# Streaming the recurrent layer's weight chunks from a contiguous DRAM copy

## The chip, the core and the metric

The kernel runs on one core of a Trainium2 chip. A time is the device time of one execution in microseconds; the time before is the median of three runs.

## The reference

Two independent parts are computed, and their outputs stand side by side in the last dimension. Part A is a shift of the keys, a long convolution by FFT, and gating. Part B, which the change touches, is a recurrent transformer: 2048 tokens in 64 segments of 32, each preceded by 8 memory tokens that the segment before has produced.

```python
for s in range(n_seg):                       # 64, strictly one after the other
    xs = x[:, s * seg_len:(s + 1) * seg_len, :]
    h = concatenate([mem, xs], axis=1)       # 40 tokens x 1024
    q, k, v = (einsum('btd,dhe->bhte', h, W) for W in (Wq, Wk, Wv))   # 32 heads x 128
    p = softmax(where(mask, q @ k.T * scale, -1e9))
    o = einsum('bhte,hed->btd', p @ v, Wo)
    mem = o[:, :8, :]                        # goes into the next segment
    outs.append(o[:, 8:, :])
```

The four weights have 1024 x 4096 elements each in bfloat16, 8 MB each and 32 MB together. They are used anew in every segment[...].

## The kernel before

`a_kernel` computes part A first, in three stages that pass data through DRAM tensors (SK1, SU1, SZ); its last stage loads `zt` tiles in turn from SP and from GpSimd (L381). Then comes `b_kernel`.

**Chunks.** The 32 MB of weights are cut into 64 chunks of 128 x 2048 elements, 512 KB each, in the order in which a segment uses them (`order`): Wk and Wq for the first half of the heads, Wk and Wq for the second, Wv for both, then Wo. A chunk of Wk, Wq or Wv is named (m, kc, g): 128 rows of the weight, and half g of its 4096 columns, so its 128 pieces of 4 KB lie 8 KB apart in DRAM. A chunk of Wo covers two heads, in pieces of 2 KB. Of the 64, 44 are resident: 18 in `Wearly` (loaded before the projection stage) and 26 in `Wlate` (loaded after it, L553). The other 20, spread evenly over the order, are *streamed*: in every segment they are fetched again from DRAM. They are 4 chunks of Wk, 6 of Wq, 5 of Wv and 5 of Wo.

**Where the stream reads.** `stream_src` (L430) gives the source. A streamed Wk, Wq or Wv chunk is read from the input itself. The five Wo chunks are first copied, in DRAM, to the scratch tensor WOS, one after the other and each contiguous (L439), by GpSimd at the very start of the run:

```python
    for i, ch in enumerate(ostream):
        nc.gpsimd.dma_start(WOS[i].rearrange("p (hh d) -> p hh d", hh=2), dram_chunk(ch))
```

**The projection stage** (L481 to L546) comes before the loop. It transposes x, and computes the keys, queries and values of the last 8 of each segment's 32 tokens for all segments at once, since these need no memory tokens, and stores them to the DRAM tensors REC and VBD. It needs Wk, Wq and Wv once in full. What is not in `Wearly` is loaded, 30 chunks in all, through the ring `pw` of ten buffers (`group`, L501). `Wlate` later takes the memory that this stage gives back.

**The segment loop** (from L590) has its order written out by hand. Projections (`Proj.run`, L649) and the output projection (`out_proj`, L735) take a resident chunk or the next one of the ring `wring`, which has four buffers. When PE has used a ring chunk, `done` calls `fetch` (L571), and SP issues the load of the chunk four places on in the stream:

```python
    def fetch():
        n = len(loaded)
        if n < len(uses):
            t = ring.tile([128, 2048], BF, tag="wring", name="wring")
            nc.sync.dma_start(t[:], stream_src(uses[n]))
            loaded.append(t)
```

So at most four fetches are under way, and one is issued only when a buffer comes free. GpSimd issues the segment's other transfers: its record `rec` (192 KB, L595), VBs (four of 16 KB, L622) and the outputs (L788, L793). After a segment PE transposes the new memory into the next one's input (L601, L602), and the next segment's projections start.

Of the kernel before, what the change touches and what calls it, by code (L numbers as in the profile page):

```python
# [9 lines left out]
BF = mybir.dt.bfloat16  # L10
# [11 lines left out]
NSTREAM = 20  # L22
NEARLY = 18
RING = 4


def a_kernel(ctx: ExitStack, tc, q, k, v, shift_k, ssm_k, ssm_D, outa, dbg_stop=None):
# [363 lines left out]
def b_kernel(ctx: ExitStack, tc, x, mem0, Wq, Wk, Wv, Wo, outb, n_seg):  # L391
    nc = tc.nc
# [11 lines left out]
    order = []  # L404
# [7 lines left out]
    streamed = set()  # L412
# [5 lines left out]
    late = resident[NEARLY:]  # L418


    ostream = [ch for ch in order if ch[0] == 3 and ch in streamed]

    def dram_chunk(ch):
        m, a, g = ch
        return Wo_v[a] if m == 3 else W_v[m][a, g]

    def dst_view(ap, ch):
        return ap.rearrange("p (hh d) -> p hh d", hh=2) if ch[0] == 3 else ap

    def stream_src(ch):  # L430
        return WOS[ostream.index(ch)] if ch[0] == 3 else dram_chunk(ch)

    dram = ctx.enter_context(tc.tile_pool(name="b_dram", bufs=1, space=DRAM))

    REC = dram.tile([128, n_seg, 768], BF, name="REC")
    VBD = dram.tile([n_seg, 4, 8, 1024], BF, name="VBD")
    WOS = dram.tile([max(1, len(ostream)), 128, 2048], BF, name="WOS")
    for i, ch in enumerate(ostream):
        nc.gpsimd.dma_start(WOS[i].rearrange("p (hh d) -> p hh d", hh=2), dram_chunk(ch))  # L439

    const = ctx.enter_context(tc.tile_pool(name="b_const", bufs=1))
    ident = const.tile([128, 128], BF, name="ident")
# [38 lines left out]
    with ExitStack() as c0:  # L481
        xp = c0.enter_context(tc.tile_pool(name="b0_x", bufs=3))
        xtp = c0.enter_context(tc.tile_pool(name="b0_xt", bufs=1))
        pring = c0.enter_context(tc.tile_pool(name="b0_ring", bufs=5))
        st = c0.enter_context(tc.tile_pool(name="b0_st", bufs=2))
        ps0 = c0.enter_context(tc.tile_pool(name="b0_ps", bufs=4, space=PSUM))
        ps0t = c0.enter_context(tc.tile_pool(name="b0_pst", bufs=2, space=PSUM))
        XT_all = xtp.tile([128, n_seg, 8, SEG], BF, name="XT_all")
        XBT = xtp.tile([128, 8, n_seg, 8], BF, name="XBT")
        for b in range(n_blk):  # L490
            X_sb = xp.tile([128, 1024], BF, tag="X_sb", name="X_sb")
            (nc.sync if b % 2 == 0 else nc.scalar).dma_start(X_sb[:], x[b * 128:(b + 1) * 128, :])
            tp = ps0t.tile([128, 1024], BF, tag="tp0", name="xt_ps")
            for kc in range(8):
                nc.tensor.transpose(tp[:, kc * 128:(kc + 1) * 128], X_sb[:, kc * 128:(kc + 1) * 128], ident[:])
            tpv = tp[:].rearrange("p (k j t) -> p j k t", k=8, j=4)
            nc.vector.tensor_copy(XT_all[:, 4 * b:4 * b + 4], tpv)
            nc.scalar.copy(XBT[:, :, 4 * b:4 * b + 4, :].rearrange("p k j t -> p j k t"), tpv[:, :, :, NX:SEG])  # L498
        nc.sync.dma_start(REC[:, :, 0:256], XT_all[:].rearrange("p s k t -> p s (k t)"))

        def group(m, g):  # L501
            ws = []
            for kc in range(8):
                ch = (m, kc, g)
                if ch in res:
                    ws.append(res[ch])
                else:
                    t = pring.tile([128, 2048], BF, tag="pw", bufs=10, name="pw")
                    nc.sync.dma_start(t[:], dram_chunk(ch))
                    ws.append(t[:])  # L510
            return ws

        flip = [0]

        def evac(dst, src):
            flip[0] ^= 1
            if flip[0]:
                nc.scalar.copy(dst, src)
            else:
                nc.vector.tensor_copy(dst, src)  # L520

        for m in (0, 1):
            for g in range(2):
                ws = group(m, g)
                stage = st.tile([128, n_seg, 16, 8], BF, tag="stage", name="stage")
                for hl in range(16):
                    ps = ps0.tile([128, 512], F32, tag="ps0", name="kb_ps")
                    for kc in range(8):
                        nc.tensor.matmul(ps[:], lhsT=ws[kc][:, hl * 128:(hl + 1) * 128],  # L529
                                         rhs=XBT[:, kc].rearrange("p s t -> p (s t)"),  # L530
                                         start=(kc == 0), stop=(kc == 7))
                    evac(stage[:, :, hl, :], ps[:].rearrange("p (s t) -> p s t", t=8))
                o = 256 * (m + 1) + 128 * g
                nc.sync.dma_start(REC[:, :, o:o + 128], stage[:].rearrange("p s h t -> p s (h t)"))
        for g in range(2):
            ws = group(2, g)
            for tb in range(4):
                vst = st.tile([128, 4, 512], BF, tag="vst", name="vst")
                for c in range(4):
                    ps = ps0.tile([128, 512], F32, tag="ps0", name="vb_ps")  # L540
                    for kc in range(8):
                        nc.tensor.matmul(ps[:], lhsT=XBT[:, kc, 16 * tb:16 * tb + 16, :].rearrange("p s t -> p (s t)"),
                                         rhs=ws[kc][:, c * 512:(c + 1) * 512], start=(kc == 0), stop=(kc == 7))
                    evac(vst[:, c, :], ps[:])
                for c in range(4):
                    nc.sync.dma_start(VBD[16 * tb:16 * tb + 16, c, :, g * 512:(g + 1) * 512], vst[:, c, :])  # L546
# [4 lines left out]
    for i, ch in enumerate(late):  # L551
        res[ch] = wlate_t[:, i, :]
        (nc.sync if i % 2 == 0 else nc.scalar).dma_start(dst_view(res[ch], ch), dram_chunk(ch))  # L553
    ring = ctx.enter_context(tc.tile_pool(name="b_ring", bufs=RING))
    one = ctx.enter_context(tc.tile_pool(name="b_one", bufs=1))
# [11 lines left out]
# [6 lines that stand above are left out]
# [33 lines left out]
    with tc.manual_schedule():  # L606
        for _ in range(RING):
            fetch()
# [190 lines left out]
def kernel(  # L799
# [24 lines left out]
    with ExitStack() as ctx_b:  # L824
        b_kernel(ctx_b, tc, B_x[0], B_mem0[0],
                 B_Wq.rearrange("d h e -> d (h e)"), B_Wk.rearrange("d h e -> d (h e)"),
                 B_Wv.rearrange("d h e -> d (h e)"), B_Wo.rearrange("h e d -> (h e) d"),
                 outb, n_seg)
# [35 lines left out]
```

## Time and profile before

| what | value |
|---|---|
| time, median of 3 runs | 2768.48 us (2750.39 to 2782.67) |
| span of the profiled execution | 2752.4 us |
| part A and the start, to about | 335 us |
| projection stage, from about 335 to | 526 us |
| Wlate loads and segment loop, from 526 us to | 2752 us |
| ring fetches | 1280, 512 KB each |
| HBM read, written | 777.14 MB, 54.00 MB |
| mean granted TensorE clock | 0.897 |

The page cuts the span in 40 slices of 68.8 us. For each slice it gives the busy share of each engine in tenths, and for the 16 DMA engines together their mean busy share and the GB/s that they moved. A wait is listed as the engine that sat idle, the tile and line of the instruction it then started, and what released it. "PE acc L649 <- DMA wring<-in_B_Wq_dram" is PE before a projection matmul, waiting for a ring chunk that comes from Wq. Ring fetches landed this long after their issue, by source: Wq 5.6 us, Wv 5.9, WOS 6.0, Wk 6.2 (medians).

### The profile page before, as it was taken

Reading aid. Unit: us, or ns where it says so; the run is one execution under the profiler, and the core shown is the slowest. Engines: PE = TensorE matmul, PEld = TensorE weight load, DVE = VectorE, ACT = ScalarE, POOL = GpSimd, SP = SyncE. Lnnn points to the kernel's source line nnn. Section 1 sums busy time; section 2 is a strip of 40 time slices with the busy share of each in tenths; the row PEclk is TensorE's granted clock in tenths of the full one; section 3 lists DMA queues with packets and bytes.
Section 4 is the critical chain, followed back from the end, with each engine's and each line's share of the span. In section 5 each row is a group of like instructions: output and inputs, shape, how many; then the busy total and the mean of one; then the engine's idle time right before and its main releaser. Section 6 shows DMA issues by size and latency. Waiting matters only on the chain. (4 is left out here: it accounts for less than half of the span.)

```text
span 2752.4 us, 76238 instructions
## 1 busy us (share of the span) xinstructions
PE 1851.6 (67%) x33620; PEld 910.9 (33%) x33620; DVE 662.9 (24%) x1944; ACT 639.9 (23%) x1143; POOL 454.2 (17%) x1195
## 2 busy tenths in 40 slices
PE   3565398556676777666666676667666767666766
PEld 1221243223333333333333333333333333333333
DVE  5896221111211111111111111111111111111111
ACT  6872111012222111112111111121212111111111
POOL 4043000001111111111111211121212111111111
PEclk9897599879999888998989988999998998998988
DMA  7986845699999998999999998999999998999897
GB/s 267 308 286 245 311 114 159 210 338 329 329 331 332 323 317 311 322 325 320 318 312 322 324 316 310 331 319 318 330 317 333 316 324 302 329 316 325 304 317 258
DMA packets 300164, 833.65 MB, mean 303 GB/s; under 512 B 72156, under 2 KB 84476, under 8 KB 299831
## 3 DMA queue, kind: packets, MB, share of 16 engines
q1 hardware_dynamic: 265560, 767.19, 79.9%
q0 software_dynamic: 23888, 37.39, 4.2%
q10 hardware_dynamic: 10384, 24.20, 2.6%
q8 instruction: 262, 4.29, 0.6%
q14 instruction: 70, 0.57, 0.1%
HBM read 777.14 MB, written 54.00 MB: 302 GB/s over the span
## 5 line engine op out<-in xcount | busy, mean ns | idle before, releaser
L649 PE MATMUL acc<-wring,rec 128*32 128x512 bf16 x3840 | 419.9, 425 | 455.5 <-DMA wring<-in_B_Wq_dram 261.0
L649 PEld LDWEIGHTS <-rec 128*32 128x32 bf16 x12288 | 341.0, 102 | 932.9 <-issue 727.9
L658 ACT CAST qkv_sb<-acc 128x512 bf16<-128x512 f32 x384 | 225.1, 586 | 1143.8 <-PE acc L649 1095.7
L649 PE MATMUL acc<-Wearly,rec 128*32 128x512 bf16 x4608 | 425.8, 451 | 34.7 <-DVE rec L602 23.6
L649 PE MATMUL acc<-Wlate,rec 128*32 128x512 bf16 x3840 | 341.3, 399 | 0.0
L735 PEld LDWEIGHTS <-OT 128*32 128x32 bf16 x8192 | 250.0, 102 | 222.9 <-issue 203.7
L735 PE MATMUL yacc<-Wlate,OT 128*32 128x256 bf16 x5632 | 280.6, 292 | 11.4 <-issue 11.4
L735 PE MATMUL yacc<-wring,OT 128*32 128x256 bf16 x2560 | 154.1, 297 | 143.8 <-DMA wring<-WOS 139.8
L626 POOL COPY KT<-rec 128x128 bf16<-128x128 bf16 x128 | 38.4, 300 | 768.2 <-PE S L675 677.9
L749 DVE COPY KT<-qk_tp 128x512 bf16<-128x512 bf16 x64 | 27.2, 425 | 549.8 <-PE qk_tp L664 549.8
L595 POOL DMA_DIRECT2D rec<-REC x64 | 37.3, 583 | 701.8 <-PE acc L649 339.1
L788 POOL DMA_DIRECT2D out_dram<-Y x64 | 48.5, 758 | 545.8 <-ACT Y L785 514.4
L622 POOL DMA_DIRECT2D VBs<-VBD x256 | 129.4, 512 | 0.2
L680 DVE TENSOR_REDUCE mx<-S 128x5 f32<-128x200 f32 x128 | 47.1, 368 | 281.9 <-PE S L675 281.1
L717 ACT CAST OT<-OTp 128x512 bf16<-128x512 f32 x128 | 75.0, 586 | 152.0 <-PE OTp L708 150.1
L664 PE MATMUL qk_tp<-ident,qkv_sb 128*128 128x128 bf16 x1024 | 110.2, 235 | 0.0
L602 DVE COPY rec<-y_tp 128x64 bf16<-128x64 bf16 x64 | 12.3, 192 | 393.0 <-PE y_tp L601 378.0
L785 ACT CAST Y<-yacc 128x256 bf16<-128x256 f32 x64 | 23.8, 373 | 356.8 <-PE yacc L735 356.8
L664 PEld LDWEIGHTS <-qkv_sb 128*128 128x128 bf16 x1024 | 63.5, 103 | 113.8 <-issue 83.8
L735 PE MATMUL yacc<-Wlate,OTB 128*32 128x256 bf16 x1408 | 91.2, 276 | 11.7 <-issue 11.3
L721 DVE CAST OTB<-OTp 128x128 bf16<-128x128 f32 x128 | 34.8, 272 | 246.3 <-ACT OT L717 246.3
L529 PE MATMUL kb_ps<-XBT,Wearly 128*128 128x512 bf16 x288 | 84.3, 384 | 1.2 <-ACT XBT L498 1.2
(191 smaller groups left out, 2131.9 us busy)
## 6 DMA issues: line engine op xcount, KB each, us to landing
wring<-in_B_Wq_dram SPq DMA_DIRECT2D x384, 512.0 KB, 5.6
wring<-in_B_Wv_dram SPq DMA_DIRECT2D x320, 512.0 KB, 5.9
wring<-WOS SPq DMA_DIRECT2D x320, 512.0 KB, 6.0
wring<-in_B_Wk_dram SPq DMA_DIRECT2D x256, 512.0 KB, 6.2
rec<-REC POOLq DMA_DIRECT2D x64, 192.0 KB, 5.7
SK<-s_sb SPq DMA_DIRECT2D x16, 512.0 KB, 4.6
SU<-s_sb SPq DMA_DIRECT2D x16, 512.0 KB, 4.9
Kg<-SK ACTq DMA_DIRECT2D x32, 256.0 KB, 3.9
```

Source lines behind the costliest of these rows:

```text
L529: nc.tensor.matmul(ps[:], lhsT=ws[kc][:, hl * 128:(hl + 1) * 128], rhs=XBT[:, kc].rearrange("p s t -> p (s t)"), start=(kc == 0), stop=(kc ...
L595: nc.gpsimd.dma_start(rec[:], REC[:, s, :])
L622: nc.gpsimd.dma_start(VBs[32 * c:32 * c + 8, :], VBD[s, c])
L626: nc.gpsimd.tensor_copy(KT[:, :, :, 32:40], KBs[:, 128 * g:128 * g + 128].rearrange("p (c i t) -> p i c t", c=4, i=4))
L649: nc.tensor.matmul(self.acc[32 * c:32 * c + 32, :], lhsT=hT[:, kc, :], rhs=w[:, c * 512:(c + 1) * 512], start=(kc == 0), stop=(kc == 7), t ...
L658: nc.scalar.copy(sb[:], self.acc[:])
L664: nc.tensor.transpose(tp[:, i * 128:(i + 1) * 128], sb[:, i * 128:(i + 1) * 128], ident[:])
L680: nc.vector.tensor_reduce(out=mx[:], in_=S, op=ALU.max, axis=AX.X)
L717: nc.scalar.copy(OT[:], o_view(g)[:, :, :, 0:32])
L721: nc.vector.tensor_copy(OTB[:, :, 4 * g:4 * g + 4, 8 * j:8 * j + 8], o_view(g)[:, :, :, 32:40])
L735: nc.tensor.matmul(yacc[32 * dq:32 * dq + 32, o:o + 256], lhsT=src, rhs=w[:, hh * 1024 + dq * 256:hh * 1024 + (dq + 1) * 256], start=(h == ...
L788: nc.gpsimd.dma_start(bass.AP(outb.tensor, outb.offset + SEG * s * 2048, [[256, 4], [2048, 32], [1, 256]]), Y[:])
```

## The change

All 20 streamed chunks get a place in one DRAM scratch tensor, WS, each chunk contiguous, and the loop streams from there alone. The Wo chunks are copied as before, now to WS. The 15 chunks of Wk, Wq and Wv are copied on the side: all of them pass through the `pw` ring of the projection stage once, and when such a tile has landed GpSimd stores it to its place in WS. The point is that the 128 pieces of 4 KB of every fetch then lie back to back in DRAM, where before those of 15 chunks lay 8 KB apart. `PITCH`, the length of a row in WS, is 2048 elements, so that rows follow each other without a gap.

```diff
+PITCH = 2048
...
-    ostream = [ch for ch in order if ch[0] == 3 and ch in streamed]
+    ring_order = [ch for ch in order if ch in streamed]
...
     def stream_src(ch):
-        return WOS[ostream.index(ch)] if ch[0] == 3 else dram_chunk(ch)
+        return WS[ring_order.index(ch), :, 0:2048]
...
-    WOS = dram.tile([max(1, len(ostream)), 128, 2048], BF, name="WOS")
-    for i, ch in enumerate(ostream):
-        nc.gpsimd.dma_start(WOS[i].rearrange("p (hh d) -> p hh d", hh=2), dram_chunk(ch))
+    WS = dram.tile([len(ring_order), 128, PITCH], BF, name="WS")
+    for ch in ring_order:
+        if ch[0] == 3:
+            nc.gpsimd.dma_start(dst_view(stream_src(ch), ch), dram_chunk(ch))
...
                 else:
                     t = pring.tile([128, 2048], BF, tag="pw", bufs=10, name="pw")
                     nc.sync.dma_start(t[:], dram_chunk(ch))
+                    if ch in streamed:
+                        nc.gpsimd.dma_start(stream_src(ch), t[:])
                     ws.append(t[:])
```

## The prediction

> **What bounds the kernel now.** I read the busy line first, then the time slices, then the waits of the segment loop, and last the transfers of single stretches. The page says that no engine is full but the DMA engines nearly are from slice 9 on:
>
> ```profile
> PE 1851.6 (67%) x33620; PEld 910.9 (33%) x33620; DVE 662.9 (24%) x1944; ACT 639.9 (23%) x1143; POOL 454.2 (17%) x1195
> ...
> DMA  7986845699999998999999998999999998999897
> GB/s 267 308 286 245 311 114 159 210 338 329 329 331 332 323 317 311 322 325 320 318 312 322 324 316 310 331 319 318 330 317 333 316 324 302 329 316 325 304 317 258
> ```
>
> The loop of 64 segments runs from 559 us (first ring fetch) to the end. Issues of the ring's Wo chunks, which close each segment, start at 584.8 us for the first of them and 2732.9 us for the last, and one segment's burst of five takes about 7 us to issue: (2148.1 - 7) / 63 = 34.0 us a segment. The waits of PE alone from 600 to 2740 us (engine, line, tile, releaser: total us, times, longest):
>
> ```profile
> PE acc L649 <- DMA wring<-in_B_Wq_dram: 260.1, 248, 3.1
> PE yacc L735 <- DMA wring<-WOS: 136.3, 177, 2.5
> PE acc L649 <- DMA wring<-in_B_Wv_dram: 94.5, 139, 2.5
> PE acc L649 <- DMA wring<-in_B_Wk_dram: 60.5, 61, 3.2
> PE yacc L735 <- issue: 30.1, 25, 2.3
> ```
>
> The first four are one wait, for a ring chunk: 551.4 us over 63 segments, 8.8 us of each 34.0. With every chunk on time a segment would need about 25 us of PE, so PE does not end the segment; the stream of 20 chunks of 512 KB does. The page's chain that ended last holds 0% on every line and is of no use here.
>
> Next: is the stream equally fast from both kinds of source? Fifteen chunks of a segment come from Wk, Wq, Wv, as 128 pieces of 4 KB with 8 KB from one to the next (half of each row of 4096 columns). Five come from WOS, the same 4 KB pieces back to back. I took windows in seven segments, five of which are shown; columns are the stretch, its length, busy time of PE, PEld, DVE, ACT, POOL, granted clock, DMA share, GB/s. First the middle of the Wk/Wq/Wv stretch, then the WOS stretch of the same segments:
>
> ```profile
> 1273.00:1296.50 23.50, 16.21 (x292) 6.77 (x293) 4.94 (x17) 5.38 (x11) 4.54 (x15) 0.93 0.91 319
> 1305.80:1328.50 22.70, 15.56 (x300) 6.49 (x300) 4.49 (x15) 5.03 (x10) 4.54 (x15) 0.98 0.96 332
> 1339.30:1362.10 22.80, 16.83 (x308) 7.04 (x311) 4.51 (x15) 5.30 (x11) 4.54 (x15) 0.93 0.93 330
> 1410.40:1433.70 23.30, 16.38 (x300) 6.77 (x293) 5.24 (x18) 5.61 (x11) 4.54 (x15) 0.93 0.94 323
> 1444.20:1468.00 23.80, 16.65 (x298) 6.77 (x302) 4.56 (x16) 4.97 (x10) 4.28 (x15) 0.93 0.89 316
> ```
>
> ```profile
> 1297.90:1304.00 6.10, 4.23 (x132) 2.97 (x127) 0.29 (x1) 1.17 (x2) 0.59 (x1) 0.93 1.01 386
> 1329.90:1338.00 8.10, 6.39 (x160) 4.24 (x163) 0.51 (x3) 1.17 (x2) 0.57 (x1) 0.79 0.88 284
> 1363.80:1370.80 7.00, 5.03 (x188) 4.16 (x182) 0.35 (x2) 1.17 (x2) 0.59 (x1) 1.00 0.91 329
> 1435.20:1441.80 6.60, 5.41 (x148) 3.77 (x146) 0.29 (x1) 1.17 (x2) 0.59 (x1) 0.74 0.94 321
> 1470.00:1475.90 5.90, 3.34 (x123) 2.25 (x116) 0.29 (x1) 0.96 (x2) 0.58 (x1) 1.00 1.00 391
> ```
>
> The reader is to divide the last column by the one before: what the engines move while they are busy. Over all seven stretches it is 321 / 0.925 = 347 GB/s in the first kind and 347 / 0.952 = 365 GB/s in the second. The trace also keeps every DMA packet. In both kinds half of the 4 KB packets take 159 ns or less, but 10.9% of those from Wk/Wq/Wv take over 200 ns against 5.0% from WOS, so the means are 187.7 and 176.8 ns. The source in HBM, not the transfer's size, makes that tail.
>
> **What the Trainium skill says.** "DMA: Bandwidth & Descriptors", section "Latency and other measured facts", has large row pitches slow copies (207 GB/s at 512 KiB, 103 at 4 MiB) and advises padding or contiguous tiles. An 8 KiB pitch is not in its list; this trace agrees in direction and is far milder, 347 against 365. The same page, "Issuing engines are not separate DMA queues": transfers of all issuers interleave on the same 16 engines. Here the loads of zt, issued in turn by SP and by POOL, land in 6.9 and 6.7 us, which agrees; so copies issued by POOL are not free where the DMA share is high. "HBM Reference", "Specifications", puts a core that streams alone at about 425 GB/s, bounded by its engines; the best stretches here show 386 to 392 at full share, so contiguous WOS has little left above it.
>
> **The change part by part.** *The stream.* All 1280 fetches keep their size, order, queue (SP) and ring of four; only the source of 960 turns from pitched to contiguous. A chunk is 128 packets on 16 engines, 8 each. If the 15 pitched chunks take on the mean of WOS: 15 x 8 x (187.7 - 176.8) ns = 1.31 us of each engine's time a segment, 84 us over 64. From the windows: 15 chunks start on average 1.73 us apart, 25.9 us, and 25.9 x (1 - 347/365) = 1.28 us, or 82 us. I take 83. It comes out of PE's 8.8 us of waiting, so PE hides none of it.
>
> *The added copies.* Fifteen of the 30 pw tiles of the projection stage are also stored to WS by POOL, 15 x 512 KB = 7.9 MB. The Wo copies were there before and only change their target. In program order three stores stand between POOL's zt loads and twelve after the identity is made. Wherever the engines are full one costs 524 KB at 316 GB/s (the rate from 260 to 345 us) = 1.66 us. pw loads were issued from 239 to 321 us for ten tiles, eight of them streamed, in stretches with DMA shares of 0.95, 1.01 and 0.81; PE's transposes at 335 us wait for X_sb loads queued there. I charge six of these eight, 10 us. The other seven fall after 362 us, where shares are 0.42 to 0.61 and PE is busy: hidden, except beside the last Wv loads at 486 to 491 us, for which PE already waits 10.2 us once; two stores there, 3 us. Sum 13 us. Bounds: 0, and all fifteen exposed, 25 us.
>
> *The added waits.* A store waits for its pw load, and behind it on POOL stand zt loads, whose ring of four already makes POOL wait 2 to 7 us for PE, and later the first rec load, for which POOL sits idle 247 us: hidden. A pw slot is free only when its store has read it; stores end a few us after the load, the slot is asked for one matmul group (about 27 us) later: hidden. Wlate, which takes over that memory, is issued from 526 us, 35 us after the last pw load: hidden. The ring's first fetch from WS is at 559 us, after all stores.
>
> Sum: 2768.5 - 83 + 13 = 2698 us, 2.5% faster.
>
> **The rivals.**
> *It is the phase, not the layout.* WOS chunks are fetched while PE does the output projection, beside fewer other transfers. For: rec and VBs loads fall in the other stretch. Against: Wk/Wq/Wv packets that start with no POOL-issued packet within 0.3 us still average 187 ns, and with 12 to 19 packets under way, where nearly all of them start, those of WOS have the shorter tail at each number. Gain 0, cost 13: 2781 us.
> *It is the place in HBM.* Mean packets of the 15 pitched positions of a segment run from 172 to 198 ns though all have one pitch, so addresses matter and the new buffer's are unknown. If WS is no better than the weights, the five Wo chunks lose too: 5 x 8 x 10.9 ns x 64 = 28 us, 2768.5 + 28 + 13 = 2809 us, slower. Against: WOS is the same layout in the same pool, and all five of its chunks are at 175 to 180.
> *The ring hides half.* SP issues a fetch only when PE has released a slot, so engines already idle 8% of the loop and may idle more: 2768.5 - 42 + 13 = 2740 us. Against: PE still waits for data in most chunks.
> *More than the packets say.* Shorter tails make all engines of a chunk end together. If all chunks follow each other as WOS chunks do now (1.61 us apart), a segment is 32.2 us, 115 us less in all: 2667 us.
>
> **How the numbers follow.** Forecast 0.52; more gain 0.10; ring hides half 0.14; phase 0.12; place 0.12. The forecast spreads by some 35 us either way (the copy's bounds, the runs before spreading over 32 us). The range reaches from just under the larger gain to the phase case, 2655 to 2785; left out is most of the place case and a little at each end. Faster by over 1% is under 2741: nearly all of the forecast, the larger gain, half of the ring case, 0.66. Slower by over 1%: the place case and a part of the phase case, 0.15. The same: 0.19.
>
> **What would show it.** Right: 34.0 us a segment falls to 32.7; PE's wait for wring falls from 551 to about 470 us; GB/s over share in the first kind of stretch rises from 347 to about 365; the WOS kind stays; the first ring fetch moves from 559 to about 572 us. Wrong: packets from WS with the old tail (place or phase), a ring fetch starting 25 us or more late (copies exposed), or the share in the loop dropping below 0.90 with the segment unchanged (ring).

## The result, and the profile after

The changed kernel takes 2680.1 us (median of 4 runs, 2659.7 to 2688.4) against 2766.7 us (2750.4 to 2782.7) before: a ratio of 0.968, 95% interval 0.960 to 0.976. The profiled executions are 2752.4 and 2686.0 us long. The one before lies near the lower end of its runs and the one after is the slowest of its four, so the pair of traces shows 66 us of the 87.

The page's slices of the changed kernel (busy share of the DMA engines in tenths, GB/s) and the start of the chain that ended last, which this time reaches back through the loop (by engine, then by line; half of the span is the ring's transfers):

```profile
DMA  7886945599999999999999999998999999999996
GB/s 282 307 285 247 345 142 162 176 370 334 332 337 330 348 319 332 338 330 328 329 334 333 329 329 334 329 326 312 330 332 329 328 349 322 346 324 346 334 345 248
...
DMA 56%; PE 31%; issue 3%; DVE 3%; ACT 1%; POOL 1%; SPq 0%; DVEq 0%; ACTq 0%; POOLq 0%
DMA wring<-WS 50%; PE acc L654 14%; PE yacc L740 6%; PE kb_ps L534 4%; PE qk_tp L669 2%; PE vb_ps L547 2%; DMA out_dram<-ot 1%; DMA Wearly<-in_B_Wk_dram 1%; ACT Y L790 1%; DMA pw<-in_B_Wv_dram 1%; PE y_tp L606 1%; DMA X_sb<-in_B_x_dram 1%; POOL Yre L342 1%; DVE rec L607 0%; DMA Wlate<-in_B_Wv_dram 0%
```

PE's waits for the ring in the loop, 600 to 2740 us:

```profile
PE acc L654 <- DMA wring<-WS: 332.1, 393, 4.3
PE yacc L740 <- DMA wring<-WS: 152.6, 197, 2.3
```

They sum to 484.7 us, 66.7 less than the 551.4 before; nearly all of the 74 us by which 63 segments got shorter (below) was waiting for chunks. The projections gained 83 us of it. The output projection, whose source was contiguous before as well, waits 16 us longer.

The segment's length is read from the copy of the output Y, once a segment. From the profile's view of tile Y, kernel before, then after (count, ns min/median/max, first and last start in us):

```profile
L785 ACT CAST Y<-yacc x64: 372/373/373, 599.1 to 2740.6; 128x256 bf16<-128x256 f32 x64
```

```profile
L790 ACT CAST Y<-yacc x64: 372/372/373, 604.5 to 2672.3; 128x256 bf16<-128x256 f32 x64
```

Divided by 63: 33.99 and 32.82 us a segment, 1.17 us less, 75 us over 64. The first segment ends 5.4 us later. The window over the loop from 700 to 2500 us (columns as in the prediction), before and after:

```profile
700.00:2500.00 1800.00, 1255.06 (x26489) 632.47 (x26480) 336.30 (x1233) 359.58 (x689) 305.26 (x904) 0.91 0.92 321
```

```profile
700.00:2500.00 1800.00, 1293.06 (x27318) 646.56 (x27319) 347.54 (x1275) 371.49 (x713) 313.58 (x935) 0.91 0.94 332
```

The reader is to see that *two* columns have moved: GB/s by 3.4%, and the share with it. GB/s over share, the figure on which the prediction was built, only goes from 349 to 353. To see why, I counted from the trace's packet records, over segments 3 to 62, how many of the 16 engines were busy at each moment (the means of packets are those of all 64 segments; "PITCH 4096" is a kernel of the experiments, with the pieces of all twenty chunks 8 KB apart):

```
                          before   after   PITCH 4096
us a segment               34.0     32.8     35.5
mean 4 KB ring packet, ns  185      182      186
  Wk/Wq/Wv chunks          188      183      186
  Wo chunks                177      180      188
us with 13 to 15 busy      12.6      9.4     13.0
us with 8 to 12 busy        4.6      2.9      7.3
engine time lost, us        3.2      2.5      4.4
```

The last row sums, over all moments with under 16 packets, the idle engines' share of 16. Packets give 20 x 8 x 2.5 ns = 0.40 us of the 1.17; most of the rest, 3.2 - 2.5 = 0.7 us, is engines that no longer stand idle while others still work. I read this as transfers that finish raggedly: a chunk has landed only when the last of its packets is done, PE frees its buffer after that, and only then is the next fetch issued. No run tests this reading by itself. What the runs do show is that waiting for PE has a part in it: where no fetch waits for PE (the run with ring and computation apart, below), 0.7 us is lost per twenty chunks, not 2.5.

### The profile page after: what moved, and what is told of

The parts are those of the page before. It is cut to its first block, busy times and chain, and to the rows that moved or that the text cites. A ratio compares the mean times of both kernels' runs of the same rounds, so it can differ in the third digit from the quotient of the medians.

```text
span 2686.0 us, 76248 instructions
## 1 busy us (share of the span) xinstructions
PE 1844.0 (69%) x33598; PEld 904.9 (34%) x33620; DVE 659.9 (25%) x1944; ACT 639.8 (24%) x1143; POOL 461.6 (17%) x1210
## 4 chain that ended last, share of the span: by engine, by line
DMA 56%; PE 31%; issue 3%; DVE 3%; ACT 1%; POOL 1%; SPq 0%; DVEq 0%; ACTq 0%; POOLq 0%
DMA wring<-WS 50%; PE acc L654 14%; PE yacc L740 6%; PE kb_ps L534 4%; PE qk_tp L669 2%; PE vb_ps L547 2%; DMA out_dram<-ot 1%; DMA Wearly<-in_B_Wk_dram 1%; ACT Y L790 1%; DMA pw<-in_B_Wv_dram 1%; PE y_tp L606 1%; DMA X_sb<-in_B_x_dram 1%; POOL Yre L342 1%; DVE rec L607 0%; DMA Wlate<-in_B_Wv_dram 0%
## 5 line engine op out<-in xcount | busy, mean ns | idle before, releaser
L654 PE MATMUL acc<-Wearly,rec 128*32 128x512 bf16 x4608 | 436.0, 461 | 32.3 <-DVE rec L607 21.3
L654 PE MATMUL acc<-Wlate,rec 128*32 128x512 bf16 x3840 | 333.3, 390 | 0.0
L740 PEld LDWEIGHTS <-OT 128*32 128x32 bf16 x8192 | 235.5, 100 | 236.2 <-issue 220.1
L740 PE MATMUL yacc<-Wlate,OT 128*32 128x256 bf16 x5632 | 274.0, 286 | 13.0 <-issue 13.0
```

The source lines that it names most:

```text
L654: nc.tensor.matmul(self.acc[32 * c:32 * c + 32, :], lhsT=hT[:, kc, :], rhs=w[:, c * 512:(c + 1) * 512], start=(kc == 0), stop=(kc == 7), t ...
L740: nc.tensor.matmul(yacc[32 * dq:32 * dq + 32, o:o + 256], lhsT=src, rhs=w[:, hh * 1024 + dq * 256:hh * 1024 + (dq + 1) * 256], start=(h == ...
```

## The experiments

**Copies without their use.** All copies as in the changed kernel, but the loop reads Wk, Wq and Wv from the weights (`ws_place` is a chunk's place in WS, to which the copies still go; those lines are left out):

```diff
-        return WS[ring_order.index(ch), :, 0:2048]
+        return ws_place(ch) if ch[0] == 3 else dram_chunk(ch)
```

> All twenty chunks are copied to WS as in the changed kernel, but the loop streams Wk, Wq and Wv from the weights and only Wo from WS. Theory 1 (the gain is made where the loop reads; the copies only cost): a segment stays at 34.0 us, the first ring fetch comes at about 566 us instead of 559, time about 2774 us, ratio to before 1.000 to 1.006. Theory 2 (the copies themselves, or the changed start of the run, bring some of the gain): ratio clearly under 0.995.

Measured: 1.0043 (1.001 to 1.0077), a segment 34.2 us, Wk/Wq/Wv packets 187 ns. Theory 1 holds: the gain is made where the loop reads. The copies and their waits cost 0.4%, 12 us, and by the interval between 3 and 21. (The 0.2 us a segment by which this trace is longer than the one before, 13 us in all, is less than the runs of one kernel differ.)

**The same scratch, other pitches.** Three kernels changed only where rows of WS lie:

```diff
-PITCH = 2048
+PITCH = 4096
```

> The changed kernel with PITCH 4096: WS has the rows of 4 KB at 8 KB from one to the next, as in the weights, in the same scratch tensor. Theory 1 (it is the layout: pieces that follow each other read with a shorter tail): the gain is gone and the Wo chunks lose theirs too, time 2780 to 2810 us, ratio 1.005 to 1.015, mean 4 KB packet about 187 ns in both kinds. Theory 2 (it is the place: the scratch tensor lies better in HBM than the weights): ratio stays at about 0.968, packets 182 ns.

```diff
-PITCH = 2048
+PITCH = 3072
```

> The changed kernel with PITCH 3072: rows of 4 KB at 6 KB, with gaps, but no power of two. If gaps as such lengthen the tail: like the 8 KB pitch, ratio near or above 1.00. If only the power of two does: like the changed kernel, ratio about 0.968. If place decides: 0.968 as well, with the 8 KB pitch also at 0.968.

```diff
-        return WS[ring_order.index(ch), :, 0:2048]
+        return WS[:, ring_order.index(ch), :]
...
-    WS = dram.tile([len(ring_order), 128, PITCH], BF, name="WS")
+    WS = dram.tile([128, len(ring_order), PITCH], BF, name="WS")
```

> WS laid out with the 128 rows outermost, so that the 4 KB pieces of a chunk are 80 KB apart and each row holds its pieces of all twenty chunks. Layout theory: at least as slow as the 8 KB pitch, ratio 1.00 to 1.03, packets 187 ns or more. Place theory: 0.968. If the tail comes from a power-of-two pitch alone (80 KB is 5 x 16 KB): between the two.

Measured: 8 KB 1.041 (1.037 to 1.045), 2867 us; 6 KB 0.977 (0.973 to 0.982); 80 KB 0.977 (0.973 to 0.981). The windows over the loop at 8, 6 and 80 KB, to be held against the two above:

```profile
700.00:2500.00 1800.00, 1226.80 (x25456) 612.32 (x25456) 322.60 (x1184) 344.29 (x661) 290.80 (x868) 0.90 0.88 308
```

```profile
700.00:2500.00 1800.00, 1283.43 (x27492) 647.38 (x27481) 348.75 (x1279) 372.67 (x715) 313.56 (x936) 0.92 0.93 333
```

```profile
700.00:2500.00 1800.00, 1288.31 (x27194) 647.19 (x27185) 343.30 (x1259) 368.02 (x706) 312.03 (x930) 0.91 0.93 331
```

At 8 KB GB/s over share is 350, the same as the kernel before; the engines simply stand idle more, 0.88. That loss, 4.1%, is larger than the 0.5 to 1.5% expected, with packets of the length expected (186 ns). Two readings are refuted here. It is not the place: the same tensor with rows at 8 KB loses all and more. And it is not contiguity: pieces with gaps of 2 KB, or 80 KB apart, are nearly as good as adjacent ones. (The intervals of 0.968 and 0.977 overlap, and the two were measured beside different runs of the kernel before; the profiled loops are 32.8, 32.7 and 33.0 us a segment.) What hurts is the 8 KB between pieces. Of the three pitches it alone is a power of two, which fits the reading that was written down for 6 KB; the 16 KB below fits it too, but no other pitches were run.

**Which part of the 8 KB layout.** Two kernels keep 8 KB between the pieces of a chunk. One puts alternate chunks into alternate halves, the other moves consecutive chunks off a spacing of exactly 1 MB:

```diff
-PITCH = 2048
+PITCH = 4096
...
-        return WS[ring_order.index(ch), :, 0:2048]
+        i = ring_order.index(ch)
+        return WS[i // 2, :, 2048 * (i % 2):2048 * (i % 2) + 2048]
...
-    WS = dram.tile([len(ring_order), 128, PITCH], BF, name="WS")
+    WS = dram.tile([len(ring_order) // 2, 128, PITCH], BF, name="WS")
```

> Rows of 4 KB at 8 KB as in the run with PITCH 4096, but two chunks share a stretch of 1 MB: the even chunk of the stream has the first half of every 8 KB, the odd one the second. Theory H (what hurts is that all chunks under way use the same 4 KB half of every 8 KB): the loss is gone, ratio 0.97 to 0.985. Theory P (the 8 KB pitch inside a chunk hurts): ratio stays at about 1.04. Theory S (chunks that lie exactly 1 MB apart hurt each other): pairs are still 1 MB apart, but only every second chunk; ratio between, about 1.00 to 1.02.

```diff
-PITCH = 2048
+PITCH = 4096
...
-    WS = dram.tile([len(ring_order), 128, PITCH], BF, name="WS")
+    WS = dram.tile([len(ring_order), 129, PITCH], BF, name="WS")
...
-        return WS[ring_order.index(ch), :, 0:2048]
+        return WS[ring_order.index(ch), 0:128, 0:2048]
```

> Rows of 4 KB at 8 KB, all in the first half, but with a spare row after each chunk, so that chunks lie 1 MB + 8 KB apart. Theory H and theory P: no help, ratio about 1.04. Theory S (1 MB apart): the loss is gone, ratio 0.97 to 0.985.

Measured: 1.027 (1.024 to 1.031) and 1.029 (1.024 to 1.033). Each takes a little over 1% off the 1.041, none comes near 0.98: theory P, the pitch inside a chunk, carries most of the loss, though it had put both at 1.04; the place of the chunks against each other carries a small part, and H and S as sole causes are refuted. No kernel has both changes at once.

**The stream by itself.** To take PE out, the loop is reduced to its fetches, with the source of the kernel before and of the changed one, and then with WS at 8 and at 16 KB (PITCH 4096 and 8192; one run each, on another chip than the first two). Part B's output is not computed.

```diff
-        OTB = None
-        for s in range(n_seg):
...
+        while used[0] < len(uses):
+            done(uses[used[0]])
```

> The kernel before without the segment loop's computation and its other transfers: after the same start, SP issues the 1280 fetches alone, each when the fetch into the same buffer four before has landed; part B's output is not computed. Theory 1 (the source's layout slows the engines by itself): a chunk takes clearly longer than in the run from WS, by 3% or more of about 1.4 us. Rival (the layout costs only through PE's releases and the other transfers): the two runs differ by under 1%.

> The same reduction of the changed kernel: 1280 fetches alone, all from WS. Theory 1: 1.33 to 1.40 us a chunk, 3% or more faster than from the pitched source, and all 16 engines busy together for a larger share of the time. Rival: within 1% of it.

> The fetches alone from WS with rows of 4 KB at 8 KB for all twenty chunks; part B's output is not computed. Theory P (the 8 KB pitch slows the engines by itself): the rate of the Wk/Wq/Wv stretch of the run with fetches alone from the weights, 364 GB/s, or a little less, 1.43 to 1.50 us a chunk. If the loss with PITCH 4096 came only through PE's releases: 408 GB/s as from the contiguous WS, 1.28 us a chunk.

> The same with rows of 4 KB at 16 KB (PITCH 8192). If a pitch that is a power of two leaves ever fewer places in HBM in use, the rate falls again, to 330 GB/s or less, 1.6 us a chunk or more. If 8 KB is special, or the loss saturates: 360 to 408 GB/s.

The windows of the four, in this order:

```profile
700.00:2300.00 1600.00, 0.00 (x0) 0.00 (x0) 0.00 (x0) 0.00 (x0) 0.00 (x0) 0.50 1.00 373
```

```profile
700.00:2200.00 1500.00, 0.00 (x0) 0.00 (x0) 0.00 (x0) 0.00 (x0) 0.00 (x0) 0.50 1.02 408
```

```profile
700.00:2300.00 1600.00, 0.00 (x0) 0.00 (x0) 0.00 (x0) 0.00 (x0) 0.00 (x0) 0.50 1.00 375
```

```profile
700.00:2300.00 1600.00, 0.00 (x0) 0.00 (x0) 0.00 (x0) 0.00 (x0) 0.00 (x0) 0.50 0.96 355
```

With nothing but fetches the layout is worth 8.6%: 28.1 us per twenty chunks from the old sources, 25.7 from WS. (A share of 1.02 is packets that overlap a little.) From WS 0.3% of the Wk/Wq/Wv packets take over 200 ns, from the weights 7.4%. Within the old sources the Wk/Wq/Wv stretch runs at 364 GB/s, Wo at 402. Pieces at 8 KB give 375, at 16 KB 355 and now with engines idle. So the layout acts on the fetches themselves, without PE's part, and a further doubling of the pitch costs more. The directions are those expected; the sizes were missed: WS needs 1.28 us a chunk and not 1.33 to 1.40, 8 KB 1.40 and not 1.43 to 1.50, and 16 KB, at 1.48, lies between its two forecasts.

**What is left.** Alone the WS stream needs 25.7 us a segment, in the kernel it takes 32.8. One run leaves out the loop's other transfers, so that all segments use the first one's record and only the last output is written:

```diff
-            VBs = one.tile([128, 1024], BF, tag="VBs", name="VBs")
-            for c in range(4):
-                nc.gpsimd.dma_start(VBs[32 * c:32 * c + 8, :], VBD[s, c])
+            if s == 0:
+                VBs = one.tile([128, 1024], BF, tag="VBs", name="VBs")
+                for c in range(4):
+                    nc.gpsimd.dma_start(VBs[32 * c:32 * c + 8, :], VBD[s, c])
...
-            if s + 1 < n_seg:
-                load_x(s + 1)
+            pend[s + 1] = (hT, KBs, QBs)
...
-            if j == NB - 1:
+            if s + 1 == n_seg:
```

> The changed kernel without the loop's transfers other than the ring: rec and VBs are loaded for the first segment alone and kept, and only the last segment's output is written. Alone the ring's chunks come at 25.7 us per twenty with packets of 163 ns, in the kernel at 32.8 us with 182 ns. Theory A (the other transfers make the rest of the tail): packets fall to 165 to 170 ns, a segment to 30.5 us or less, ratio to before 0.92 or less. Theory B (PE's releases with a ring of four, and the on-chip traffic of the computation, make it): only the moved bytes are saved, about 1.1 us of engine time a segment at most, packets stay over 177 ns, ratio 0.94 to 0.97.

Measured: 0.946 (0.941 to 0.951), 31.6 us a segment, packets 183 ns. Theory B: their own bytes are saved, 1.2 us a segment, and the tail stays.

The other lets stream and computation run side by side without waiting for each other; PE multiplies by resident chunks in place of the streamed ones:

```diff
-        return loaded[used[0]]
+        return res[early[used[0] % 18]]
```

> The changed kernel with the ring and the computation taken apart: all 1280 fetches run with four under way, but PE multiplies by resident Wearly chunks in their place, so that it never waits for the ring and the ring never for PE; the other transfers stay. Theory B1 (the rest of the tail and the loss come from the mutual waits of PE and the ring): fetches run at 25.7 to 27 us per twenty, packets at 163 to 168 ns, PE needs about 25 us a segment, time about 2250 us. Theory B2 (the computation beside the stream lengthens packets by itself): packets 175 ns or more and twenty fetches take 28 us or more although nothing waits.

Measured: 0.889 (0.883 to 0.895). The computation ends at 2130 us, the stream goes on alone; the window up to 2100 us and one after it:

```profile
700.00:2100.00 1400.00, 1176.69 (x28544) 641.63 (x28536) 361.64 (x1331) 387.45 (x743) 326.13 (x969) 0.95 0.99 367
2200.00:2400.00 200.00, 0.00 (x0) 0.00 (x0) 0.00 (x0) 0.00 (x0) 0.00 (x0) 0.50 1.03 409
```

Nothing waits for the ring here, yet twenty fetches take 30.0 us and their packets 175 ns, until the computation ends: then 25.7 us and 163 ns. PE's own pace is (2130.1 - 587.2) / 63 = 24.5 us a segment. By time B2 is right and B1 covers the remainder: of the 7.1 us between 25.7 and 32.8, 4.3 come with the computation and its transfers running beside the stream, and 2.8 from PE and the ring waiting for each other. The split is that of this run: its computation goes a third faster than in the changed kernel, and so puts more beside each fetch.

Two more things stand in the packet records. In this run, ring packets that start with no packet of another queue under way, nor within 0.3 us after one, average 171 ns, the others 178: the GpSimd transfers and the instruction fetches, which the page lists as DMA queues of their own, account for a part of the 12 ns and not for most of it. And in the changed kernel the packets that start with at least 15 others under way average 175 ns, those with fewer 213 (172 and 203 here). Long packets and idle engines come together; which makes which is not shown.

## Why the prediction was right, and where it was not

**What bounds the kernel** was read rightly. PE needs 24.5 us a segment when it never waits for a chunk, where the text worked out about 25; the ring stream sets the pace.

**The stream's gain** came out near its sum, 1.31 us a segment forecast and 1.17 measured in the traces (about 1.5 by the medians: 87 us, and the 12 that the copies cost), but the term was wrong inside, and that the sum came near is in part luck. "If the 15 pitched chunks take on the mean of WOS" did not come about: their packets went from 188 to 183 ns and not to 177, while the Wo chunks, unchanged in layout, rose from 177 to 180. That is 0.40 us, a third of the forecast. The rest came from idle engines, which the prediction held constant, and which the rival "the ring hides half" even took to grow. The share in the loop rose instead, from 0.92 to 0.94. GB/s over share divides exactly this part out, so the windows agreed with the packets at 82 and 84 us only because both looked at the same half of the effect. Seven segments were also too few: over segments 3 to 62 the Wk/Wq/Wv stretch had moved 310 GB/s at a share of 0.90, not 321 at 0.925; after the change it has 327 at 0.93. GB/s over share went there from 344 to 351, not to the 365 named as a sign of being right.

**"The source in HBM, not the transfer's size, makes that tail"** holds only in part. The pitch lengthens packets with no computation at all, but a contiguous stream, with 0.3% long packets alone, has 7.5% in the kernel.

**The added copies** were charged at 13 us, and the copies without their use cost 12 by their ratio, which its wide interval makes a weak test. The traces are a better one. From the first zt load to the REC store behind the x loads, 95.3 and 95.7 us pass in the two traces without the copies, and 104 to 110 in the twelve with them, 106 in the changed kernel: some 10 us, as charged for the part beside the x loads. The 3 us beside the last Wv loads did not appear: from that store to the first Wlate load it is 191 to 195 us with the copies and 191 and 193 without. (The first ring fetch of the changed kernel comes only 6.6 us later, at 566.0 in place of 559.4 and not at about 572, because its zt loads happened to start 3 us earlier, at 234.8 in place of 237.9.)

**The rivals.** The phase is refuted by the 8 KB pitch in the same kernel. The place is refuted as the cause of the gain, though moving chunks against each other did shift the 8 KB kernel by over 1%. The cause that the change and the prediction gave, that pieces should be contiguous, is corrected: adjacent, 6 KB or 80 KB apart all do; 8 KB does not. "The ring hides half" did not happen: the share rose and PE's waits fell. "More than the packets say" pointed at the part that the forecast lacked, engines that idle less, and only put it too high, at 32.2 us a segment against 32.8; whether the engines of a chunk then end together, as it says, was not tested.

"So addresses matter", read from positions that range from 172 to 198 ns, needs care: with all chunks contiguous the fifteen positions still range from 172 to 208 in the kernel, and alone they are all at 163 or 164, so the kernel makes such a spread without any difference of layout. Alone the old sources do spread, from 163 to 205, and three of the fifteen pitched positions are at 163 like a contiguous chunk. The 8 KB pitch is thus needed for the loss, but does not slow every fetch; which ones it slows was not found.

**Open.** Alone, WS at 8 KB is as fast as the old sources (28.0 and 28.1 us per twenty chunks); in the kernel it is slower, 35.5 against 34.0 us. By the table most of it is idle engines, 4.4 us lost against 3.2, and the five Wo chunks that lost their contiguous place, 188 ns against 177, are a part; the rest was not separated. What in the computation lengthens the packets that start beside no other queue, 171 ns against 163 alone, was not tried. No kernel with a deeper ring was run.

## What to carry to other kernels

When a loop is bound by a stream of weights, ask how far apart the pieces of one transfer lie, and measure the stream alone with both layouts; here rows of 4 KB at 8 KB, in three quarters of the chunks, cost 8.6% of the stream's rate alone and 3% of the kernel, and a copy made once, while the data passed by on another errand, cost about 12 us to win about 99 (87 and the 12, by the medians). Read the rate of busy engines *and* the share of time in which they are busy: here the second carried more of the gain than the first. And expect a part only of what the stream alone gains: of 2.4 us a segment, 1.2 arrived in the traces.

## What was not expected of the hardware

Rows of 4 KB at 6 KB or at 80 KB read about as well as adjacent ones in the kernel, while 8 KB and, with fetches alone, 16 KB fall from 408 to 375 and 355 GB/s. The Trainium skill ("DMA: Bandwidth & Descriptors", "Latency and other measured facts") lists such losses from a pitch of 512 KiB on, where its copies still reach 207 GB/s of a full 214; these runs show them far below that pitch, and at 8 KB already larger than that 3%, so "far milder" in the prediction holds only against the larger pitches of that list. And a computation with its transfers beside a stream, with no wait between them, lengthened the stream's 4 KB packets from 163 to 175 ns.
